# Last pass of a retention and two-MLP kernel: matmuls in the order of the source, and the squared Relu on ScalarE

## The chip, the cores and the metric

One core of one Trainium2 chip runs the whole program. The metric is device time in microseconds (us), the median of several runs.

## The reference, cut to what matters

```python
# q, k, v: (4, 8, 576, 64); 2304 tokens, width 512
ret = (scale * q @ k.T) * decay_mask        # retention, no softmax
x   = (ret @ v) -> (2304, 512)
x   = (silu(x @ w_gate) * (x @ w_val)) @ w_out     # hidden width 1536
h   = x @ w_in                                      # (2304, 2048)
g   = np.maximum(h, 0.0) ** 2                       # the squared Relu
out = g @ moe2_w_out                                # (2304, 512)
```

All matrices are float32. The kernel splits each operand into a rounded high part and a low rest, and forms each product from three matmuls (high-high, high-low, low-high).

## The kernel before, in words

After the retention, the two MLPs run in **passes** over blocks of tokens: two passes for the first, three for the second (`TOKENS`). The change touches the **last pass** of the second MLP, 768 tokens, which is the loop `for n in range(turn_over, end + 1)` (L1103).

**Systems and slots.** A pass goes through the hidden width in eight systems of 256 hidden columns. The products with `w_in` are done in Winograd-Strassen fashion: seven products instead of eight, numbered 1 to 7. One product of one system is a **slot**: six matmuls of 384 columns (`product`, L630). Products 1, 6, 7 and 4 of a system build up in one PSUM bank (`g`), 5 and 3 in another (`v`), 2 in a third (`z`). ScalarE copies a bank out between two products that share it, so product 4 can't begin before the copy after product 7 is done. The last pass has 59 slots: three that belong to the system before it, and 56 of its own. Products 7, 4 and 3 of a system stand one iteration behind its 1, 2, 6 and 5 in `seq` (L1105): 1 of n, 7 of n-1, 2 of n, 4 of n-1, 6 of n, 3 of n-1, 5 of n.

**The squared Relu** of a system stands behind products 2, 4 and 3: on 384, 384 and 768 columns. VectorE does it as one instruction, max(x, 0) times x; behind product 4, whose value lies in PSUM, ScalarE makes a Relu first.

**Block products.** In the first three pairs of systems of this pass, the second product (with `w_out`) is again done in seven products for each of three blocks of 128 tokens: 3 pairs x 3 token blocks x 7 = 63 **block products**, each six matmuls of 256 columns (`out3`, L885). Their sums of hidden blocks are four GpSimd instructions for each token block (`sums2`), which begin when the Relu behind product 3 of the pair's second system is done; `prepare` then rounds them (ScalarE, tile `hs_h`) and takes the rest (VectorE, `hs_l`). Their operands (tiles `wt`, 256 KB each) come by DMA from `operands2`. The tiles of the second pair take the place of the first pair's: a load waits until the third token block has used the tile. Block products use two PSUM banks in turn, and each bank is added into `xy` (by VectorE, or for some products of the first pair copied by ScalarE) before it is written again. The last pair of systems ends in six plain output tiles of twelve matmuls with 512 columns (`out4`; the last of them in two halves).

**Order.** Every engine executes its queue in order. The order is set when the program is built: a scheduler takes the instructions in the order of the source, and moves one ahead where, by its own estimate of times, an earlier one would have to wait. `Chained` (L109) can forbid this: while `chain["on"]` holds, each instruction of an engine is queued behind the one before it. In the kernel before this holds for the retention alone. In the last pass the source lets 1.5 block products follow each slot, from slot `begin_at` = 21 + `START` on (`flow`, L1095 and L1135), but the scheduler may place them elsewhere.

Of the kernel before, what the change touches and what calls it, by code (L numbers as in the profile page):

```python
# [13 lines left out]
AF = mybir.ActivationFunctionType  # L14
ALU = mybir.AluOpType
# [41 lines left out]
PRODUCTS = (1, 5, 6, 3, 7, 2, 4)  # L57
SUMS = (6, 5, 4, 7)
PAIRED = 6
START = 4  # L60


TINY = float(np.uint32(0x38000000).view(np.float32))
# [4 lines left out]
def retention_moe_kernel(  # L68
# [38 lines left out]
    chain = {"on": False}  # L107

    class Chained:  # L109


        def __init__(self, engine):
            self.engine, self.last, self.recent = engine, None, None

        def __getattr__(self, name):
            op = getattr(self.engine, name)

            def traced(*args, **kw):
                with ExitStack() as behind:
                    if self.last is not None:  # L120
                        behind.enter_context(tc.issue_after(self.last))
                    i = op(*args, **kw)  # L122
                self.recent = i.ins
                if chain["on"]:
                    self.last = i.ins
                return i

            return traced

    pe, dve, act, pool_e, sp = map(Chained, (nc.tensor, nc.vector, nc.scalar, nc.gpsimd, nc.sync))  # L130
# [140 lines left out]
    def bank(tag):  # L271

        turn[tag] += 1
        home = ps_g2 if late and turn[tag] % 2 else ps_g
        return home.tile([P, 512], F32, tag=tag, name=tag)
# [52 lines left out]
    def temp(tag, rows):  # L328
        return (c4_p if tag[1] == "g" else c4m_p).tile([P, rows, M1], F32, tag=tag, name=f"c{tag}", bufs=1 + (tag[1] == "g"))
# [300 lines left out]
    def product(n, dst, first, *which):  # L630

        for x, (i, o) in enumerate(which):
            w = built[n, i]
            for c in range(2):
                hi, lo = (w[:, y, c * P:(c + 1) * P] for y in range(2))
                xh, xl = (z[:, c] for z in xo[o])
                for j, (a, b) in enumerate(((hi, xh), (hi, xl), (lo, xh))):
                    at = (x * 2 + c) * 3 + j
                    pe.matmul(
                        dst, a, b, start=first and at == 0, stop=at == 6 * len(which) - 1, skip_group_check=True  # L640
                    )

    def plain_slot(n, r):
# [13 lines left out]
        if r:  # L657
            hidden(n, "c", gc)

    def slot(n, i):  # L660

        ph, p, k, what = systems[n]
        m = M[ph]
        s = sys_.setdefault(n, {})

        if i == 1 and n >= turn_over:
            s["x"] = bank("g")[:, :m]
            s["a"], s["b"] = block_tiles(n)
        elif i == 1:
            s["x"] = bank("g")[:, :m]  # L670
            s["a"] = temp("av" if what == "v" else "ag", 1 + (what != "v"))[:, :, :m]
            s["b"] = temp("bv" if what == "v" else "bg", 2)[:, :, :m]
        if i == 5:
            s["y"] = bank("v")[:, :m]
        if i == 2:
            s["z"] = ps_a.tile([P, 512], F32, tag="a0", name="z")[:, :m]
        x, a, b = s["x"], s["a"], s["b"]
        product(n, s[{2: "z", 5: "y", 3: "y"}.get(i, "x")], i in (1, 2, 5), (i, i))
        relu2 = dict(scalar=0.0, op0=ALU.max, op1=ALU.mult)
        silu = dict(func=AF.Silu)  # L680
        if what == "v":
            ga, gb = sys_[n - 1]["a"], sys_[n - 1]["b"]
        if i == 1:
            act.copy(a[:, 0], x)
        elif i == 6:
            act.copy(b[:, 0], x)
        elif i == 7:
            act.copy(b[:, 1], x)
            tt(out=b[:, 1], in0=s["y"], in1=b[:, 1], op=ALU.add)
        elif i == 2:  # L690
            tt(out=a[:, 0], in0=s["z"], in1=a[:, 0], op=ALU.add)
            if what == "g":
                act.activation(out=a[:, 0], in_=a[:, 0], **silu)
            elif what == "v":
                tt(out=ga[:, 0], in0=a[:, 0], in1=ga[:, 0], op=ALU.mult)
            else:
                dve.scalar_tensor_tensor(out=a[:, 0], in0=a[:, 0], in1=a[:, 0], **relu2)
        elif i == 4:
            if what == "g":
                act.activation(out=a[:, 1], in_=x, **silu)  # L700
            elif what == "v":
                tt(out=ga[:, 1], in0=x, in1=ga[:, 1], op=ALU.mult)
                hidden(n, "a", ga)
            else:
                act.activation(out=a[:, 1], in_=x, func=AF.Relu)
                dve.scalar_tensor_tensor(out=a[:, 1], in0=x, in1=a[:, 1], **relu2)
                hidden(n, "a", a)
        elif i == 3:
            tt(out=b[:, 0], in0=s["y"], in1=b[:, 0], op=ALU.add)
            if what == "g":  # L710
                act.activation(out=b, in_=b, **silu)
            elif what == "v":
                tt(out=gb, in0=b, in1=gb, op=ALU.mult)
                hidden(n, "b", gb)
                del sys_[n - 1], sys_[n]
            else:
                dve.scalar_tensor_tensor(out=b, in0=b, in1=b, **relu2)
                hidden(n, "b", b)
                del sys_[n]

# [2 lines left out]
    def hidden(n, which, c):  # L723
        if n >= turn_over:
            return
        kw = dict(bufs=2) if n > flip - 1 and which == "a" else {}
        hi = ho_p.tile(list(c.shape), F32R, tag=f"h{which}", name="ho_hi", **kw)
        lo = ho_p.tile(list(c.shape), F32R, tag=f"l{which}", name="ho_lo", **kw)
        split(hi, lo, c)
        hid[n, which] = hi, lo  # L730
# [67 lines left out]
    def block_tiles(n):  # L798

        k = systems[n][2]  # L800
        if k % 2 == 0:
            home = block_pools[k // 2 % 2]
            pairs_of[n] = pairs_of[n + 1] = [
                home.tile([P, 2, 2, M[2]], F32, tag=f"g{x}", name=f"ca{x}") for x in "ab"
            ]
        return [x[:, k % 2] for x in pairs_of[n]]
# [148 lines left out]
    flip, turn_over = systems.index((2, 0, 0, "i")), systems.index((2, 2, 0, "i"))  # L955
# [139 lines left out]
    def flow(upto):  # L1095
        while flowed["n"] < min(upto, len(stream)):
            follow(*stream[flowed["n"]])
            flowed["n"] += 1

    slots["n"] = 0  # L1100
    make2 = iter(())
    begin_at = 7 * 3 + START
    for n in range(turn_over, end + 1):  # L1103
        tiles = outs.get(n, [])
        seq = [(1, n), (7, n - 1), (2, n), (4, n - 1), (6, n), (3, n - 1), (5, n)]  # L1105
        if n == turn_over:
            seq = [(7, n - 1), (4, n - 1), (3, n - 1), None, (1, n), (2, n), (5, n), (6, n)]
        make = build(n + 1) if n + 1 < end else iter(())
        for x in fetch.get((n, 0), []):
            load_out(*x)  # L1110
        for x in seq:
            if x is None:
                blocks.close()
                block_pools.append(pool(ctx, "ca_p", 1, side="right"))
                t1_p = pool(ctx, "t1_p", 1, side="right")
                make2 = operands2(n + 1)
                continue
            i, k = x
            if k == end:
                continue  # L1120
            slot(k, i)
            if i == 3 and k >= turn_over and systems[k][2] % 2:
                for j in range(3):
                    if k < turn_over + PAIRED:
                        sums2(k, j)
                    queue.append((k, j))
                ready_halves()
            next(make, None)
            if tiles and (n == turn_over or i in (7, 4, 3)):
                fn, *args = tiles.pop(0)  # L1130
                fn(*args)
            slots["n"] += 1
            next(make2, None)
            past = slots["n"] - begin_at
            flow(min(int(1.5 * past + 0.7 * max(0, past - 28)), 21 * PAIRED // 2))  # L1135
            if past == 1:
                make2 = operands2(turn_over + 2)
            after(k, i)
            if n == turn_over + 1 and not tiles and t_p is None:
                second.close()  # L1140
                t_p, hl_p = pool(ctx, "t_p", 1), pool(ctx, "hl_p", 2)
                block_pools.append(pool(ctx, "cb_p", 1, side="right"))
        for fn, *args in tiles:
            fn(*args)
        for _ in make:
            pass
        if n == turn_over:
            for _ in make2:
                pass
        if n == end - 1:  # L1150
            load_last(n)
# [62 lines left out]
```

## Time and profile before

| | us |
|---|---|
| median of 3 runs | 877.3 (876.49 to 878.25) |
| the profiled execution | 876.15 |
| its span in the profile | 874.3 |
| TensorE busy in the span | 862.4 (99%) |
| VectorE busy | 675.5 (77%) |
| ScalarE busy | 415.8 (48%) |
| GpSimd busy | 172.4 (20%) |

The profiled execution took 1.85 us outside of its span. The rows of the profile call TensorE's matmuls PE, its weight loads PEld, VectorE DVE, ScalarE ACT, GpSimd POOL, and SyncE's queue of transfers SPq. All instructions go through a helper, so they all carry line 122; they are told apart by their tiles. The duration of a matmul is modelled and longer than the distance to the next one, since matmuls overlap: a wait that is shorter than this overlap doesn't show as idle time.

### The profile page before, as it was taken

To read this page: it belongs to the slowest core of one execution; us is meant where nothing else is said; L and a number is where in the kernel's file an instruction comes from. 1 tells how busy PE (TensorE), PEld (TensorE's weight loads), DVE (VectorE), ACT (ScalarE), POOL (GpSimd) and SP (SyncE) were. 2 spreads that over 40 slices of the span, in tenths; PEclk is the share of its full clock that TensorE was granted. 3 is DMA by queue.
4 is the path that set the end of the run, shared out by engine and by line. 5 is a ranking of instruction groups with operands and counts; after the bars stand their busy time and mean duration, and the time that the engine had idled before them with its cause. 6 is when DMAs were issued, how large, how long until landed. Compare 5 with 4: busy or idle time off the path is not lost.

```text
span 874.3 us, 14199 instructions
## 1 busy us (share of the span) xinstructions
PE 862.4 (99%) x5226; PEld 751.1 (86%) x5226; DVE 675.5 (77%) x1082; ACT 415.8 (48%) x756; POOL 172.4 (20%) x195
## 2 busy tenths in 40 slices
PE   8999999999999999999999999999999999999998
PEld 7878888888888888888888999889899988999986
DVE  3799999998976998778647999999654566457783
ACT  3677768564553554634335466554244232234321
POOL 3343243123220000000002311132211000062400
PEclk9999999999999999999999999999999999999999
DMA  9994867655653589878744498999989755666432
GB/s 335 402 377 158 280 231 270 243 199 174 217 197 129 175 296 365 304 252 295 249 146 156 165 338 319 357 319 385 386 286 333 250 207 157 222 236 199 164 119 72
DMA packets 87029, 217.81 MB, mean 249 GB/s; under 512 B 8752, under 2 KB 24112, under 8 KB 86960
## 3 DMA queue, kind: packets, MB, share of 16 engines
q1 hardware_dynamic: 86528, 216.50, 70.2%
q8 instruction: 41, 0.67, 0.3%
q10 hardware_dynamic: 432, 0.41, 0.1%
q14 instruction: 28, 0.23, 0.1%
HBM read 146.10 MB, written 70.78 MB: 248 GB/s over the span
## 4 chain that ended last, share of the span: by engine, by line
PE 82%; DVE 7%; DMA 7%; issue 2%; ACT 1%; SPq 0%; DVEq 0%; ACTq 0%
PE oacc L122 40%; PE g L122 24%; PE v L122 12%; PE z L122 6%; DMA k_sb<-in_kv 3%; DVE w L122 3%; DMA wt<-tsp 2%; DMA qk_sb<-in_qk 1%; DVE wi L122 1%; DVE xy L122 1%; DVE xo_l L122 1%; DMA v_sb<-in_kv 1%; DVE hs_l L122 0%; DVE cbg L122 0%; PE o L122 0%
## 5 line engine op out<-in xcount | busy, mean ns | idle before, releaser
L122 PE MATMUL g<-xo_h,wi 128*128 128x384 f32 (+1 forms) x768 | 241.3, 364 | 0.0
L122 PEld LDWEIGHTS g<-xo_h,wi 128*128 128x128 f32 x768 | 142.6, 188 | 16.8
L122 DVE TENSOR_TENSOR xy<-oacc,xy 128x512 f32<-128x512 f32 (+1 forms) x194 | 112.2, 585 | 54.2 <-PE oacc L122 53.5
L122 PE MATMUL oacc<-ho_hi,wo 128*128 128x512 f32 (+1 forms) x480 | 151.1, 370 | 0.5 <-ACT xy L122 0.5
L122 PE MATMUL g<-xo_l,wi 128*128 128x384 f32 (+1 forms) x384 | 139.7, 364 | 0.0
L122 PE MATMUL v<-xo_h,wi 128*128 128x512 f32 (+1 forms) x384 | 124.6, 364 | 0.0
L122 PE MATMUL oacc<-wo,ho_hi 128*128 128x512 f32 x384 | 119.8, 392 | 0.0
L122 PEld LDWEIGHTS oacc<-ho_hi,wo 128*128 128x128 f32 x480 | 88.1, 188 | 17.6 <-ACT xy L122 1.3
L122 PE MATMUL oacc<-ho_lo,wo 128*128 128x512 f32 (+1 forms) x240 | 89.1, 371 | 0.0
L122 PEld LDWEIGHTS oacc<-wo,ho_hi 128*128 128x128 f32 x384 | 71.5, 188 | 12.1
L122 DVE TENSOR_SCALAR w<-w 128x512 f32<-128x512 f32 (+1 forms) x136 | 65.4, 483 | 18.4 <-ACT w L122 17.4
L122 PEld LDWEIGHTS g<-xo_l,wi 128*128 128x128 f32 x384 | 72.1, 188 | 8.6
L122 PEld LDWEIGHTS v<-xo_h,wi 128*128 128x128 f32 x384 | 71.4, 188 | 8.2
L122 PE MATMUL oacc<-wo,ho_lo 128*128 128x512 f32 x192 | 74.3, 393 | 0.0
L122 PE MATMUL v<-xo_l,wi 128*128 128x512 f32 (+1 forms) x192 | 69.9, 364 | 0.0
L122 PE MATMUL z<-xo_h,wi 128*128 128x512 f32 (+1 forms) x192 | 63.0, 365 | 0.0
L122 PEld LDWEIGHTS oacc<-ho_lo,wo 128*128 128x128 f32 x240 | 45.1, 188 | 8.7
L122 ACT ACTIVATE raw<-raw 128x512 uint32<-128x512 uint16 x68 | 46.0, 677 | 13.5 <-DMA raw<-in_w 9.4
L122 DVE SCALAR_TENSOR_TENSOR w<-raw,w 128x512 uint32<-128x512 uint32 x68 | 51.2, 754 | 0.7
L122 DVE CUSTOM_DVE_ANT_0 w<-raw,w 128x1024 uint16<-128x1024 uint16 x68 | 48.7, 716 | 0.8
L122 PE MATMUL oacc<-wt,hs_h 128*128 128x256 f32 x252 | 46.9, 286 | 1.7 <-DVE xy L122 0.6
L122 DVE TENSOR_TENSOR cbg<-v,cbg 128x384 f32<-128x384 f32 (+1 forms) x56 | 34.1, 609 | 18.0 <-PE v L122 10.3
(119 smaller groups left out, 1531.6 us busy)
## 6 DMA issues: line engine op xcount, KB each, us to landing
wi<-win SPq DMA_DIRECT2D x84, 512.0 KB, 5.1
raw<-in_w SPq DMA_DIRECT2D x68, 512.0 KB, 4.8
win<-wi SPq DMA_DIRECT2D x60, 512.0 KB, 3.8
wo<-wsp SPq DMA_DIRECT2D x32, 512.0 KB, 6.0
wsp<-wo SPq DMA_DIRECT2D x28, 512.0 KB, 5.3
qk_sb<-in_qk SPq DMA_DIRECT2D x15, 576.0 KB, 7.2
wst<-w SPq DMA_DIRECT2D x32, 256.0 KB, 6.2
wi<-win SPq DMA_DIRECT2D x28, 256.0 KB, 5.9
```

The source lines that it names most:

```text
L122: i = op(*args, **kw)
```

## The change

Three things change together, all in the last pass:

- every TensorE instruction of the pass is queued behind the one before it in the source (`pe.on`)
- the squared Relu there is two ScalarE instructions, Relu and Square (`square`); VectorE has none of it
- block products begin two slots later in the source (`START` 4 to 6), and the pace at which they follow the slots is written otherwise

```diff
-START = 4
+START = 6
...
-                if chain["on"]:
+                if chain["on"] or self.on:
                     self.last = i.ins
...
+    def square(n, dst, src):
+        late_ = n >= turn_over
+        if late_ or src is not dst:
+            act.activation(out=dst, in_=src, func=AF.Relu)
+        if late_:
+            act.activation(out=dst, in_=dst, func=AF.Square)
+        else:
+            dve.scalar_tensor_tensor(out=dst, in0=src, scalar=0.0, in1=dst, op0=ALU.max, op1=ALU.mult)
...
-                dve.scalar_tensor_tensor(out=a[:, 0], in0=a[:, 0], in1=a[:, 0], **relu2)
+                a0 = a[:, 0]
+                square(n, a0, a0)
...
-                act.activation(out=a[:, 1], in_=x, func=AF.Relu)
-                dve.scalar_tensor_tensor(out=a[:, 1], in0=x, in1=a[:, 1], **relu2)
+                square(n, a[:, 1], x)
...
-                dve.scalar_tensor_tensor(out=b, in0=b, in1=b, **relu2)
+                square(n, b, b)
...
     slots["n"] = 0
+    pe.on, pe.last = True, pe.recent
...
             past = slots["n"] - begin_at
-            flow(min(int(1.5 * past + 0.7 * max(0, past - 28)), 21 * PAIRED // 2))
+            flow(min(int(1.5 * past + 0.25 * max(0, past - 14) + 0.45 * max(0, past - 26)), 21 * PAIRED // 2))
```

## Rows read from the trace of the kernel before

**Rows 1.** The page, part 1: busy time of each engine and its share.

```profile
PE 862.4 (99%) x5226; PEld 751.1 (86%) x5226; DVE 675.5 (77%) x1082; ACT 415.8 (48%) x756; POOL 172.4 (20%) x195
```

**Rows 2.** Stages of the last pass: length, busy time (instructions) of each engine, clock, DMA.

```profile
718.20:780.00 61.80, 61.80 (x332) 57.41 (x331) 35.87 (x52) 19.16 (x36) 9.91 (x12) 1.00 0.62 206
780.00:833.30 53.30, 52.31 (x360) 51.45 (x359) 37.49 (x67) 19.08 (x39) 19.82 (x24) 1.00 0.56 182
833.30:871.00 37.70, 36.17 (x230) 31.65 (x228) 23.12 (x46) 7.18 (x12) 0.00 (x0) 1.00 0.26 86
871.00:874.30 3.30, 0.00 (x0) 0.00 (x0) 0.40 (x1) 0.00 (x0) 0.00 (x0) 1.00 0.26 77
```

**Rows 3.** One tile's instructions in a stretch: `wi`; `wt`; `wo`; `wt` from 833.3.

```profile
765.50:871.00 105.50, 41.14 (x218) 36.91 (x216) 0.00 (x0) 0.00 (x0) 1.00 0.48 160
...
765.50:871.00 105.50, 51.30 (x378) 48.37 (x378) 1.00 0.48 160
...
765.50:871.00 105.50, 17.50 (x84) 14.05 (x84) 0.00 (x0) 0.00 (x0) 0.00 (x0) 1.00 0.48 160
...
833.30:871.00 37.70, 18.93 (x144) 17.67 (x144) 1.00 0.26 86
```

**Rows 4.** The chain that ended last, in order of time: start, length, what.

```profile
789.94 2.09 PE g L122 x12
792.02 1.42 PE oacc L122 x12
...
802.31 7.16 DMA wt<-tsp
...
809.53 7.30 DMA wt<-tsp
```

**Rows 5.** Timeline of PE: start, length, instruction, matmuls merged, idle time before.

```profile
816.11 0.28 PE L122 MATMUL oacc<-wt,hs_l 128*128 128x256 f32 x1
816.88 0.38 PE L122 MATMUL oacc<-wt,hs_h 128*128 128x256 f32 x1 [0.49 <-DMA wt<-tsp]
...
858.13 0.63 PE L122 MATMUL oacc<-wo,hs_h 128*128 128x512 f32 x2
...
858.83 0.63 PE L122 MATMUL oacc<-wo,hs_h 128*128 128x512 f32 x2
```

**Rows 6.** Timeline of four engines: from slot product 3 to the first block sums.

```profile
763.27 0.33 PE L122 MATMUL v<-xo_h,wi 128*128 128x384 f32 x1
...
765.00 0.95 DVE L122 SCALAR_TENSOR_TENSOR cab<-cab 128x768 f32<-128x768 f32 x1
...
767.68 1.05 POOL L122 TENSOR_TENSOR xy<-cab 128x256 f32<-128x256 f32 x1
...
769.58 0.73 POOL L122 TENSOR_TENSOR xy<-cab 128x256 f32<-128x256 f32 x1
...
773.06 2.89 POOL L122 TENSOR_TENSOR xy<-caa,xy 128x256 f32<-128x256 f32 x3
...
774.58 2.00 ACT L122 CAST hs_h<-xy 128x1024 fp32r<-128x1024 f32 x2 [0.66 <-POOL xy L122]
...
775.67 1.36 DVE L122 TENSOR_TENSOR hs_l<-xy,hs_h 128x1024 fp32r<-128x1024 f32 x1 [1.72 <-ACT hs_h L122]
```

**Rows 7.** Instruction groups of one shape: count, busy us, mean ns, idle before.

```profile
L122 DVE SCALAR_TENSOR_TENSOR cab<-cab 128x768 f32<-128x768 f32 x8 | 7.6, 956 | 0.2
L122 DVE SCALAR_TENSOR_TENSOR caa<-caa 128x384 f32<-128x384 f32 x8 | 5.3, 662 | 0.1
...
L122 ACT CAST xo_h<-xy 128x768 fp32r<-128x768 f32 x4 | 3.3, 834 | 2.4 <-DVE xy L122 1.6 <-PE v L122 0.8
L122 ACT ACTIVATE caa<-g 128x384 f32<-128x384 f32 x8 | 3.9, 493 | 10.7 <-PE g L122 10.7
...
L122 ACT ACT_TABLE_LOAD x2 | 2.6, 1283 | 2.2 <-issue 2.2
```

**Rows 8.** Waits of SP's queue from 765.5: sum, times, longest.

```profile
SPq L122 <- PE oacc L122: 31.4, 13, 8.7
```

More of the change, by code (lines that the diff above doesn't have):

```diff
@@ L112, in __init__ @@
         def __init__(self, engine):
-            self.engine, self.last, self.recent = engine, None, None
+            self.engine, self.last, self.recent, self.on = engine, None, None, False
         def __getattr__(self, name):
@@ L678, in slot @@
         product(n, s[{2: "z", 5: "y", 3: "y"}.get(i, "x")], i in (1, 2, 5), (i, i))
-        relu2 = dict(scalar=0.0, op0=ALU.max, op1=ALU.mult)
         silu = dict(func=AF.Silu)
```

## The prediction

> **What bounds the kernel now.** I read the page's first part, then busy time by stage, then the last pass on TensorE's own timeline. TensorE is busy for 99% of the span [rows 1], so only two things can change the time: the amount of its work, and the time in which it stands still. The change leaves its work alone; the question is what it stands still for, before and after. In the last pass it shows no idle time up to 780, then 1.0 us to 833.3 and 1.5 us to 871; the 3.3 us behind that are the last addition and its store [rows 2]. These idle times understate the loss, because a matmul's modelled end lies behind the start of the next. So I count the loss by starts. Twelve matmuls of 384 columns take 2.09 us, 0.174 each, and twelve of 256 take 1.42, 0.118 each [rows 4]; three of 512 take 0.70, 0.233 each [rows 5]. From 765.5 there are 216 of the first kind (36 slots; the row shows two more that began at its edge), 378 of the second (all 63 block products), and 84 in the output tiles, of which 60 have 512 and 24 have 256 columns [rows 3]. Work: 216 x 0.174 + (378 + 24) x 0.118 + 60 x 0.233 = 37.6 + 47.4 + 14.0 = 99.0 us. It runs from 765.5 to about 870.8, 105.3 us. **Lost: 6.3 us.** I put it at 6.1, since waits alone count. Of this, the tail from 833.3 holds the most: 144 matmuls of block products [rows 3], which is 24 of the 63, and the output tiles make 17.0 + 2.8 + 14.0 = 33.8 of 37.5 us, so 3.7 are lost there and some 2.4 before it. One such loss is seen at 816.88: the matmul starts 0.77 us after the one before it, where 0.12 is normal, behind a transfer of `wt` [rows 5].
>
> **The change part by part.** *The order.* By the source, 55 block products stand ahead of slot 59, with the old pace (past = 34: 51 + 0.7 x 6) as with the new (past = 32: 48 + 4.5 + 2.7). The scheduler had put only 39 there, and 24 into the tail. In the order of the source 8 are left for the tail. That moves no work away, but a block product between slots has a slot's 1.04 us more until its bank is needed again, and one in the tail has only the 0.71 us of its neighbour. With 8 in place of 24 in the tail, the 3.7 us lost there would shrink to 1.2 in proportion; the products of neighbouring token blocks are also no longer mixed, so that rounding of the next block can begin one block product group earlier. I take 0.8, bounds 0 and 1.5.
>
> *The start of the block products* is where the new order can cost. The second block product needs a sum that hangs on slot product 3 of the second system (slot 20). Block product 1 follows slot 28 (21 + 6 + 1) and the second follows slot 29. From the modelled end of slot 20's last matmul that is nine slots and one block product, 9.4 + 0.7 less the 0.16 us of overlap: TensorE arrives after 9.95 us. The chain that it needs: an addition of 384 columns (0.6 with its wait, by the 384-column row of VectorE), Relu and Square on 768 columns (0.83 each by ScalarE's rounding of that size [rows 7]), 0.2 of hand-overs, so GpSimd starts at 2.5. It started 2.35 us after that matmul in the trace [rows 6] (763.60 to 765.95), so the second ScalarE step costs nothing beyond what VectorE's queue cost there. Then GpSimd: its twelve instructions were queued with the three token blocks interleaved, so the first block's sums were complete only with the tenth. ScalarE could round them at 774.58, 8.6 us after 765.95 [rows 6]. Some of those instructions took 1.05 us and others 0.73 [rows 6]; ten at 0.72 would be 7.2. Then 1.05 for rounding, and the rest 1.3 later, of which 0.24 hides. So TensorE waits 2.5 + 7.2 + 1.05 - 9.95 = 0.8 for the high part and 1.05 more for the low one, 1.9 us in all; with 8.6 it is 3.3, and with the blocks one after the other (four instructions, 2.9) the chain is done at 7.8 and nothing waits. In the kernel before other slots were put into this gap, which the new order forbids. I take 2.0, bounds 0 and 3.3: nearest to the undisturbed rows, because VectorE loses its squaring. Rows show the longer GpSimd instructions while such VectorE work ran at 765.00 and just after [rows 6]. The Trainium skill (GPSIMD Engine Reference, Specifications) says that GpSimd shares its SBUF interfaces with VectorE and contends with VectorE instructions that have two SBUF inputs; the squaring is one. By that rule alone the wait is 1.9, without it 3.3; the trace agrees as far as 1.05 against 0.73 us goes.
>
> *Operands of the next pair.* A `wt` tile is loaded again when the third token block has used it. Between that and its next use the source has about four slots and five block products, 4.2 + 3.5 + 0.4 = 8.1 us. Two such transfers took 7.16 and 7.30 us from release to use [rows 4]. That fits with half a microsecond to spare; bounds 0 and 1.5 (twice the 0.65 us lost at 816.88), taken 0.5.
>
> *Product 7 to product 4.* Without block products between them only one slot, 1.04 us, covers ScalarE's copy: 0.16 of overlap, about 0.1 to start, 0.5 for 384 columns [rows 7]. This leaves some 0.3, and two or three times the copy may stand behind a Relu or Square of 0.83 us: 0 to 1, taken 0.2.
>
> *Squared Relu.* VectorE loses 8 instructions of 0.96 and 16 of at most 0.66 us, some 18 us. ScalarE gains five of them for each system, 2 x 0.83 + 3 x 0.49 = 3.1 us, 25 in all. It was busy 45 of 153 us [rows 2], so both lie under TensorE and cost nothing by themselves; without this cover, on a chain that TensorE waits for, each square would cost 0.1 (behind product 4) to 0.7 us (behind 3).
>
> **The sum.** New waits 2.0 + 0.5 + 0.8 + 0.2 = 3.5, old ones 6.1: 2.6 us less. The profiled execution took 876.15 (span 874.3 and 1.85 around it), so 873.55. That execution was 1.15 below the median of 877.3; against the median I forecast **874.7 us**. From no change I count what differs by over 0.2%, 1.75 us, about what a measurement of this kernel can tell.
>
> **Rivals.**
> - *The waits go altogether.* The sums are ready in time, and the tail runs through: new waits 0.5 to 1. 877.3 - 5.5 = 871.8 us. For it: the bounds of 0 above. Against: the interleaved sums were seen [rows 6].
> - *They only move.* At the first block products 3.3, and the other terms at their upper bounds of 1.5, 1.5 and 1: 7.3 in place of 6.1, 878.5; halfway there, 876 to 878: no change. That the scheduler's order was already that of the source I rule out nearly (39 products against 55); it would give 877.3.
> - *Slower: one late transfer.* SP issues transfers in order, and its queue stood up to 8.7 us for a block product [rows 8]. TensorE may no longer pass over a block product whose `wt` is late. If a load stands 8.7 us behind another's wait, its half microsecond of slack leaves 8.2 us of standing still: 877.3 + 8.2 - 2.6 = 882.9. It decides from 4.4 us of such lateness on (2.6 + 1.75). Against: by the source the loads stand in the order in which tiles come free.
> - *Slower: function tables.* A load of ScalarE's tables took 1.28 us, and there were two in the whole kernel [rows 7], none between the Silu and the Relu that the last pass used already. If Square needed other tables than Relu and copy, each of 24 Squares would bring two loads, 62 us on ScalarE, and a copy that has 0.3 us to spare would stand behind them: at 1 us each, 877 + 24 = some 900. The Trainium skill (ScalarE: Activation LUTs, Table sets) says that functions lie in sets, and that a switch of set costs a load of about 1283 ns and a DRAIN; cheap functions are in every set, where its list names relu, copy, identity and abs but not square. No row of this trace has a Square.
>
> **How the numbers follow.** Forecast 0.50, waits gone 0.14, only moved 0.20 (with the order unchanged in it), a late transfer 0.14, tables 0.02. Of the forecast's half, 0.04 lies above 875.55, the bound of no change, and of the moved case 0.01 above 879.05. So faster 0.60, same 0.23, slower 0.17. The range leaves out the last two cases and little of the second: 871.9 to 878.7. The likeliest case's own range is 873 to 876.
>
> **What would show it.** In the timeline of the changed kernel: slots and block products strictly alternating, 8 block products behind the last slot in place of 24; a wait of about 2 us at the second block product, released by `hs_h` or `hs_l`; less than 1 us lost in the tail; GpSimd's instructions near 0.73; no squaring on VectorE; two table loads as now. I am wrong if the first wait is over 4 us, if PE waits several times for `wt`, or if a third table load appears.

## The result, and the profile after

| | before | after |
|---|---|---|
| median, us | 877.58 (876.49 to 878.25, 4 runs) | 884.62 (884.3 to 885.68, 4 runs) |
| the profiled execution / its span | 876.15 / 874.3 | 884.61 / 882.8 |

The changed kernel is **slower**: ratio 1.0084, 95% interval 1.0066 to 1.0101. I had forecast 874.7 us, a range of 871.9 to 878.7, and given "slower" 0.17.

Busy time of the whole kernel after the change, as in [rows 1]:

```profile
PE 864.4 (98%) x5226; PEld 752.5 (85%) x5226; DVE 657.5 (74%) x1058; ACT 437.8 (50%) x796; POOL 168.3 (19%) x195
```

The work moved as planned: VectorE lost 18 us, ScalarE gained 22, TensorE's instructions are as many as before. The stages, with the same columns as [rows 2]:

```profile
718.20:780.00 61.80, 57.12 (x294) 51.65 (x292) 28.60 (x42) 27.43 (x48) 8.70 (x12) 1.00 0.62 200
780.00:833.30 53.30, 49.05 (x340) 47.84 (x341) 26.64 (x48) 26.04 (x53) 13.08 (x17) 1.00 0.51 168
833.30:879.50 46.20, 45.75 (x296) 42.23 (x294) 26.51 (x52) 15.72 (x26) 5.06 (x8) 1.00 0.34 104
```

Where [rows 2] showed no idle time up to 780 and 1.0 us to 833.3, 4.7 and 4.25 us are now idle; the tail has 0.45 in place of 1.5. As in the prediction, idle time alone understates the loss, so I also count by starts: in the profiled execution, how much later than at the normal pace (0.174, 0.119 and 0.232 us behind a matmul of 384, 256 and 512 columns) each matmul of the last pass starts, summed. This "lost" time is **5.8 us before and 12.4 after**, in four stretches:

| lost, us | 718 to 765 | 765 to 800 | 800 to 833.3 | from 833.3 |
|---|---|---|---|---|
| before | 0.1 | 1.4 | 0.9 | 3.6 |
| after | 0.1 | 8.7 | 2.5 | 1.6 |

So the tail gained 2 us (I expected 2.9, from 3.7 to 0.8), and 765 to 833.3 gave back 8.9. (The stretches are counted each with its own pace; they add up to 0.2 and 0.5 more than the whole.) The two spans differ by 8.5 us, of which 1.9 arose ahead of this pass: matmul 4301, in order of start, begins at 716.2 before and at 718.1 after. That leaves 6.6 us for the last pass, as the count does (12.4 - 5.8). The view of waits says for what TensorE stood still from 718 on, in us, times, longest:

```profile
PE g L122 <- ACT caa L122: 3.7, 2, 2.9
PE g L122 <- DMA wi<-win: 3.1, 1, 3.1
PE oacc L122 <- ACT hs_h L122: 0.8, 1, 0.8
PE oacc L122 <- DVE hs_l L122: 0.8, 1, 0.8
PE oacc L122 <- DMA wt<-tsp: 0.4, 1, 0.4
PE oacc L122 <- DVE xy L122: 0.3, 1, 0.3
```

Before, the longest such wait was 0.5 us. The places, on TensorE's timeline (columns as in [rows 5]):

```profile
772.69 0.44 PE L122 MATMUL g<-xo_h,wi 128*128 128x384 f32 x1 [3.12 <-DMA wi<-win]
...
778.65 0.50 PE L122 MATMUL oacc<-wt,hs_h 128*128 128x256 f32 x2 [0.80 <-ACT hs_h L122]
779.91 0.38 PE L122 MATMUL oacc<-wt,hs_l 128*128 128x256 f32 x1 [0.76 <-DVE hs_l L122]
...
790.26 0.45 PE L122 MATMUL g<-xo_h,wi 128*128 128x384 f32 x1 [2.90 <-ACT caa L122]
```

I call them **A** (772.69), **B** (778.65 and 779.91) and **C** (790.26, and once more 1.0 us at 823.01). The chain that ended last, in order of time, shows what stands behind each:

```profile
764.39 8.25 DMA wi<-win
...
772.69 1.31 PE g L122 x6
774.00 1.05 PE v L122 x6
...
775.08 0.57 DVE cab L122
...
775.67 0.85 ACT cab L122
...
776.55 0.85 ACT cab L122
777.39 0.26 ACT xy L122
777.65 0.95 ACT hs_h L122
...
778.63 1.24 DVE hs_l L122
```

*A.* Product 3 of the second system ends at 764.37 and frees a tile of `wi`. The load into it is issued at once and lands 8.25 us later. Product 6 of the fourth system needs it, and in the written order only five slots (5.2 us) lie between. So TensorE stands for 8.25 - 5.2 = 3.05 us, and 0.06 for the two hand-overs. The free order of the kernel before had other slots and twelve matmuls of block products to put there.

*B.* The second block product waits for the rounding of its sums. That cast ran only at 777.65: behind Relu, Square (`cab`) and a copy in ScalarE's queue, which had themselves waited for product 3 of the third system, late by A.

*C.* ScalarE's timeline around 790:

```profile
787.27 0.62 ACT L122 CAST hs_h<-caa 128x512 fp32r<-128x512 f32 x1
787.80 0.52 ACT L122 ACTIVATE caa<-caa 128x384 f32<-128x384 f32 x1
788.22 0.35 ACT L122 COPY xy<-oacc 128x256 f32<-128x256 f32 x1
788.48 0.40 ACT L122 CAST hs_h<-cab 128x256 fp32r<-128x256 f32 x1
788.78 1.04 ACT L122 CAST hs_h<-xy 128x1024 fp32r<-128x1024 f32 x1
789.73 0.48 ACT L122 COPY caa<-g 128x384 f32<-128x384 f32 x1
```

Product 6 of the fifth system can't begin before product 1 is copied out of its bank into `caa` (789.73). This `caa` still holds the first pair's hidden values, until the third token block is rounded (787.27). The rounding needs a pair of `hs` tiles, of which there are two; one comes free when the first token block's seventh block product is done, at 787.25. Since block products now begin two slots later, so does this release, and the copy stands behind it in ScalarE's queue.

### The profile page after: what moved, and what is told of

Its sections match the earlier page's. It is cut to its first block, busy times and chain, and to the rows that moved or that the text cites. A ratio compares the mean times of both kernels' runs of the same rounds, so it can differ in the third digit from the quotient of the medians.

```text
span 882.8 us, 14205 instructions
## 1 busy us (share of the span) xinstructions
PE 864.4 (98%) x5226; PEld 752.5 (85%) x5226; DVE 657.5 (74%) x1058; ACT 437.8 (50%) x796; POOL 168.3 (19%) x195
## 4 chain that ended last, share of the span: by engine, by line
PE 83%; DMA 7%; DVE 6%; ACT 2%; issue 1%; SPq 0%; DVEq 0%
PE oacc L122 40%; PE g L122 23%; PE v L122 12%; PE z L122 6%; DVE w L122 3%; DMA qk_sb<-in_qk 2%; DMA wt<-tsp 2%; PE o L122 2%; DMA v_sb<-in_kv 1%; PE s L122 1%; DMA wi<-win 1%; DMA raw<-in_w 1%; DVE wi L122 1%; DVE xy L122 1%; PE kv L122 1%
## 5 line engine op out<-in xcount | busy, mean ns | idle before, releaser
L122 PEld LDWEIGHTS oacc<-wo,ho_hi 128*128 128x128 f32 x384 | 71.5, 188 | 12.4
```

## The experiments

Each batch ran beside the kernel before on the same chip; its medians were 876.7 to 877.5. "Lost" is that of the profiled execution's last pass. That execution isn't always near the median: it took 889.03 with the order fixed from slot 28, 882.87 with the squares alone and 882.55 with START 4.

| run | median, us | ratio, 95% interval | lost, us |
|---|---|---|---|
| fixed order alone | 886.76 | 1.0102 (1.0073 to 1.0131) | 14.2 |
| squares on ScalarE alone | 880.64 | 1.0042 (1.0025 to 1.0059) | 9.8 |
| START and pace alone | 877.96 | 1.0012 (1.0001 to 1.0024) | 6.4 |
| order, START and pace | 887.35 | 1.0114 (1.0093 to 1.0135) | 16.8 |
| change, 3 ahead of 6 | 878.98 | 1.0015 (1.0001 to 1.0030) | 6.6 |
| change, START 4 | 884.90 | 1.0077 (1.0051 to 1.0103) | 11.8 |
| change, fixed from slot 28 | 885.77 | 1.0083 (1.0057 to 1.0110) | 15.7 |
| before, fixed from slot 57 | 879.84 | 1.0024 (1.0011 to 1.0038) | 7.9 |
| change, 6 last | 877.47 | 0.9995 (0.9982 to 1.0007) | 5.4 |
| change, 6 last, START 8 | 880.48 | 1.0035 (1.0022 to 1.0048) | 9.3 |
| 3 ahead of 6, squares on VectorE | 880.18 | 1.0039 (1.0021 to 1.0057) | 9.1 |
| before, 3 ahead of 6 | 878.33 | 1.0014 (1.0001 to 1.0027) | 6.8 |
| change, sums in order | 884.87 | 1.0075 (1.0048 to 1.0101) | 13.5 |
| change, 6 last, sums in order | 877.01 | 0.9994 (0.9980 to 1.0009) | 4.7 |
| the same, copies on VectorE | 875.53 | 0.9977 (0.9961 to 0.9993) | 4.1 |
| before, sums in order | 875.68 | 0.9982 (0.9967 to 0.9997) | 3.6 |
| before, sums in order, squares on ScalarE | 877.81 | 1.0007 (0.9991 to 1.0022) | 5.6 |
| before, sums in order, 6 last | 878.25 | 1.0007 (0.9992 to 1.0022) | 5.3 |

**The parts of the change.** The first four undo parts of it. My theories were A, the fixed order makes the loss, and B, ScalarE's queue does (in these four expectations the letters name theories, not the waits).

```diff
# fixed order alone: START 4, old pace, and squares on VectorE
-        late_ = n >= turn_over
+        late_ = False
# squares alone: START 4, old pace, and no fixed order
-    pe.on, pe.last = True, pe.recent
# START and pace alone: both of these edits, START 6 and the new pace
# order, START and pace: late_ = False alone
```

> TensorE's matmuls of the last pass in the order of the source; squared Relu on VectorE and the block products' pace as before. Theory A (the fixed order makes the loss: a slot waits for a wi load, the first block products for their sums, a slot for ScalarE's copy into a hidden tile that an earlier pair still occupies): 3 to 7 us slower than before, 880.5 to 884.5, with single PE waits of 2 to 3.5 us between 768 and 795. Theory B (the loss is ScalarE's queue, which got 25 us of Relu and Square): 873 to 877, no wait over 1.5 us.

> Squared Relu of the last pass in two ScalarE instructions; order left to the scheduler, pace as before. Theory A: within 1 us of before, 876.5 to 878.5. Theory B: 4 to 7 us slower, 881.5 to 884.5.

> Only START 6 and the new pace; order left to the scheduler, squares on VectorE. Both theories: within 1.5 us of before, since the scheduler moves block products anyway; if it is slower by over 2 us, the later start is a cause of its own.

> Order of the source and the new pace, squares on VectorE: the change without its ScalarE part. Theory A: 4 to 7 us slower than before, 881.5 to 884.5, close to the whole change. Theory B: 873 to 876. A value between, 878 to 881, would say that both share the loss.

The fixed order alone costs 1.0%, START and pace 0.1%, the squares alone 0.4%. The order alone, and order with pace, lie 2.3 and 2.9 us above even theory A's ranges. The order alone has the waits A (3.0 us) and B (2.7), and no C. Much of the rest is TensorE's clock: between 765 and 800 the granted clock was 0.85 in the profile of the order alone and 0.90 with order and pace, where the changed kernel had 1.00. Over the whole span, three executions of the order alone at a clock of 0.993 to 0.995 took 886.75 to 887.17, and one at 0.999 took 881.49; with order and pace, three at 0.996 took 886.72 to 887.97, and one at 1.000 took 883.90. By these executions 3 to 5 us of the two medians is the lower clock, which came in or just behind the waits.

The parts don't add up: with order and pace in place, the squares on ScalarE seem to give back 2.7 us (887.35 to 884.62, though the two intervals overlap) instead of costing 3.7. But at a clock of 1.000 the two kernels took 883.90 and 884.30, one execution each, so the 2.7 us may be the clock alone. Neither theory holds alone, but the order is the largest part.

The 2 us that the tail gained need both edits. From 833.3 on, 3.9 and 3.5 us are lost in the two runs with the fixed order and squares on VectorE, 4.0 with the squares on ScalarE and a free order, 3.6 before, and 1.6 with both. These stretches hold unlike work, since in the fixed order the last slots run until 854 to 857. Behind the last slot alone, 3.5 us are lost before, 1.8 in both runs with the fixed order and squares on VectorE, 3.7 with the squares alone, and 0.8 with both edits. The waits of the run with order and pace, whose matmuls stand in the same written order as the changed kernel's, are for VectorE's additions, and a square stands ahead of them in VectorE's queue, of 384 columns (and the rest of 1024 columns before it) at the first and of 768 at the second:

```profile
855.03 0.51 PE L122 MATMUL oacc<-wt,hs_h 128*128 128x256 f32 x2 [0.79 <-DVE xy L122]
859.04 0.50 PE L122 MATMUL oacc<-wt,hs_h 128*128 128x256 f32 x2 [0.55 <-DVE xy L122]
```

```profile
852.96 1.22 DVE L122 TENSOR_TENSOR hs_l<-xy,hs_h 128x1024 fp32r<-128x1024 f32 x1
854.10 0.55 DVE L122 SCALAR_TENSOR_TENSOR caa<-g,caa 128x384 f32<-128x384 f32 x1
...
857.70 0.96 DVE L122 SCALAR_TENSOR_TENSOR cab<-cab 128x768 f32<-128x768 f32 x1
858.58 0.75 DVE L122 TENSOR_TENSOR xy<-oacc,xy 128x256 f32<-128x256 f32 x2
```

In the run with the squares alone TensorE shows one long wait, for a transfer, and nothing of ScalarE:

```profile
817.74 0.50 PE L122 MATMUL oacc<-wt,hs_h 128*128 128x256 f32 x2 [3.44 <-DMA wt<-tsp]
```

That transfer took 9.37 us, where two like it took 7.16 and 7.30 [rows 4]; behind the wait TensorE ran at the lower clock for 3.4 us.

**Short distances in the written order.** From here on, theory C says that each wait is a distance in that order that is too short; theory D, that the order has no slack anywhere, so that what is won at one place is lost at the next.

```diff
# change, 3 ahead of 6
-        seq = [(1, n), (7, n - 1), (2, n), (4, n - 1), (6, n), (3, n - 1), (5, n)]
+        seq = [(1, n), (7, n - 1), (2, n), (4, n - 1), (3, n - 1), (6, n), (5, n)]
# change, 6 last
+        seq = [(1, n), (7, n - 1), (2, n), (4, n - 1), (3, n - 1), (5, n), (6, n)]
# change, START 4: with the old pace
-START = 6
+START = 4
# change, fixed from slot 28 (57 in the other run, with START 4, old pace, squares on VectorE)
-    pe.on, pe.last = True, pe.recent
...
             slots["n"] += 1
+            if slots["n"] == 28:
+                pe.on, pe.last = True, pe.recent
```

> The whole change, with product 3 of the system before put one slot ahead of product 6 in each iteration (order 1, 7, 2, 4, 3, 6, 5). Theory C (each wait is a distance in the written order that is too short): the tile wi1 that product 3 frees is needed by product 6 seven slots later instead of five, 2.1 us more, so the 3.3 us wait at 772.7 falls to about 1.2; the sums behind product 3 begin one slot earlier, so the 2.0 us at the second block product fall to about 1.0; product 6 of the fifth system comes one slot later, so the 3.1 us at 790.3 fall to about 2.0. Together 4 us less than the whole change: about 880.6. Theory D (the order has no slack anywhere, so time won at one place is lost at the next): waits in other places grow, total within 1.5 us of the whole change, 883 to 886.

The first gave 5.6 us back, more than the 4 expected. Its waits:

```profile
773.24 0.44 PE L122 MATMUL g<-xo_h,wi 128*128 128x384 f32 x1 [1.63 <-DMA wi<-win]
777.74 0.50 PE L122 MATMUL oacc<-wt,hs_h 128*128 128x256 f32 x2 [0.36 <-ACT hs_h L122]
779.00 0.38 PE L122 MATMUL oacc<-wt,hs_l 128*128 128x256 f32 x1 [0.76 <-DVE hs_l L122]
789.35 0.44 PE L122 MATMUL g<-xo_h,wi 128*128 128x384 f32 x1 [0.43 <-ACT caa L122]
```

A fell by 1.5 rather than 2.1 (its transfer took 8.84 us this time), C by 2.5 and its second wait of 1.0 is gone, the others fell by a little.

> The whole change, with products in the order 1, 7, 2, 4, 3, 5, 6: product 3 is as early as in the run with 3 ahead of 6, and product 6 is one slot later still. Theory C: the wait for wi1 falls by one more slot, from 1.8 us to about 0.8; the two at the second block product stay at 1.4 together, since product 3 has not moved; the wait for caa, 0.6, goes. Together 1.6 us less than with 3 ahead of 6: about 877.4. Theory D: product 6 now stands only one slot ahead of product 7 of its system, and the copy out of the bank between them waits behind the squares: several waits of 0.3 to 1 us, 879 or more.

With product 6 one slot later still, the time was 877.47 for 877.4 expected, and A and C are gone from its timeline. B stayed (1.0 and 1.0, for 1.4 expected), and a new wait of 1.3 came at 798.06:

```profile
773.63 0.50 PE L122 MATMUL oacc<-wt,hs_h 128*128 128x256 f32 x2 [0.84 <-ACT hs_h L122]
775.01 0.39 PE L122 MATMUL oacc<-wt,hs_l 128*128 128x256 f32 x1 [0.88 <-DVE hs_l L122]
798.06 0.51 PE L122 MATMUL oacc<-wt,hs_h 128*128 128x256 f32 x2 [1.13 <-ACT xy L122]
```

So two products moved in the written order, with nothing else touched, take away the whole loss of the change.

> The whole change, but block products begin two slots earlier (START 4, with the old pace). Theory C: the wait for wi at 772.7 stays at 3.3; the wait at the second block product grows by two slots, from 2.0 to about 4; the wait of product 6 of the fifth system for the copy into caa falls by as much, from 3.1 to about 1, and the 1.0 us at 823 goes; total 0 to 1 us below the whole change, 883.5 to 885. Theory D: the sum of the waits grows with the earlier start, 886 to 888, since nothing of the first wait is given back.

C vanished, B grew to 3.4 us and A stayed at 3.1, as theory C says (about 4 was expected for B). The total was within its 883.5 to 885, but in part by luck: A, B and C together are 2.8 us shorter than in the changed kernel, and a granted clock of 0.51 between 776.3 and 783.2 took most of that back. START trades one wait for another:

```profile
771.04 0.44 PE L122 MATMUL g<-xo_h,wi 128*128 128x384 f32 x1 [2.93 <-DMA wi<-win]
776.58 0.80 PE L122 MATMUL oacc<-wt,hs_h 128*128 128x256 f32 x2 [2.46 <-ACT hs_h L122]
777.84 0.58 PE L122 MATMUL oacc<-wt,hs_l 128*128 128x256 f32 x1 [0.47 <-DVE hs_l L122]
```

> The same order 1, 7, 2, 4, 3, 5, 6, with block products beginning two slots later still (START 8). Theory C: the waits at the second block product (1.4) go; the wait for caa comes back, since the first group of block products ends two slots later: 2.1 us less the slack of about 0.4, so 1.6. The two edits cancel: within 1 us of the run with START 6, 876.5 to 878.5. If the copy into caa has more slack than that, about 876.

In this kernel the second pair's sums stand in the source ahead of the rounding of a token block of the first pair, which is then computed from the wrong sums; the amount of work is the same. B went and C came back, 2.0 us for 1.6 expected. The total of 880.48 lies 2 us above the bound, with a new wait of 1.6 us for `hs_l` at 830.69, so it doesn't confirm the sum.

> The whole change, but the fixed order of TensorE begins only behind the 28th slot, where the block products begin; the slots ahead of it are free to be moved. Theory C: the wait for wi1 at 772.7 (3.3 us) is the only one that goes, since the scheduler can put other slots ahead of product 6; the waits at the second block product (2.0) and for caa (3.1) stay: about 881.3. Theory D: the time comes back at the second block product, which is reached 3 us earlier while its sums are no earlier: about 884.

> The kernel before, with one thing added: the fixed order of TensorE from slot 57 of the last pass on (squares on VectorE, START 4 and the old pace as before). Theory C: none of the three places with a short distance lies there, so no wait of over 1 us is added; the tail is in order and loses about 1 us less than before: 875 to 877. Theory D: a fixed order of even these last slots costs more than it saves: 878 to 880.

For theory C both were misses. With the order fixed from slot 28 on, A shrank to 0.6, but B grew to 3.3 and C stayed; the rest is TensorE's clock (below). This is what theory D says of B. Fixing the order from slot 57 on, with the squares on VectorE, made the kernel before slower by 0.2%, as theory D expected; from 833.3 on it lost 5.5 us for 3.6, in six waits of 0.35 to 0.9 us and smaller ones. The fixed order is thus no gain in the tail by itself.

> The kernel before with only the order of products 3 and 6 changed (no fixed order, START 4, squares on VectorE). Theory C: the scheduler already fills the gap in front of product 6 with other slots, so the distance costs nothing there: 876 to 878, no change. If the short distance also cost the kernel before something (a share of the 2.4 us lost ahead of 833), it gains up to 2 us: 875.

With a free order the same exchange gains nothing (1.0014): the scheduler had covered A already.

> Product 3 ahead of product 6, the fixed order and START 6 with the new pace, but the squares on VectorE as before. With the old order of products, moving the squares to ScalarE was worth 2.7 us (887.35 against 884.62). If that came from TensorE's clock, which fell to the lower level behind the long waits of the kernel with squares on VectorE, it vanishes here, where no wait is over 2 us: 878 to 880. If VectorE itself was late, the 2.7 us stay: 881 to 882.

880.18 lies just above the 878 to 880 of the clock, 1.2 us above the run with squares on ScalarE, within the two intervals. The profiles' tails differ as above, 4.5 us lost for 1.5 from 833.3 on, without a fall of the clock in either, so the clock is not all that the squares were worth.

**The order of the sums.** GpSimd's queue is put in the source's order, so that the first token block's four sums come first.

```diff
     slots["n"] = 0
+    pool_e.on, pool_e.last = True, pool_e.recent
# copies on VectorE
         if k == 1 and i in (1, 5, 6, 4):
-            act.copy(home, src)
+            dve.tensor_copy(out=home, in_=src)
```

> The whole change, with GpSimd's instructions of the last pass also queued in the source's order, so that the four sums of the first token block come first instead of mixed with those of the other two. If the 2.0 us at the second block product come from the mixing: the first block's sums are done after 2.9 instead of 7.2 us, both waits there go, and the rest stays (3.3 for wi1, 3.1 for caa): about 882.6. If they come from ScalarE's queue (rounding behind Relu, Square and a copy): no change, 884 to 885.

B went completely, and yet the time stayed. TensorE's two remaining long waits, and the three windows behind them (length, busy times, granted clock as the third number from the end):

```profile
771.97 0.45 PE L122 MATMUL g<-xo_h,wi 128*128 128x384 f32 x1 [3.19 <-DMA wi<-win]
789.02 0.45 PE L122 MATMUL g<-xo_h,wi 128*128 128x384 f32 x1 [2.90 <-ACT caa L122]
```

```profile
772.00:775.00 3.00, 3.00 (x11) 3.00 (x12) 0.47 (x1) 1.31 (x2) 3.00 (x4) 0.62 0.35 143
775.00:778.00 3.00, 3.00 (x17) 3.00 (x17) 1.69 (x2) 1.27 (x4) 0.87 (x2) 0.81 0.44 119
790.00:793.00 3.00, 3.00 (x15) 3.00 (x14) 0.31 (x1) 1.68 (x4) 0.00 (x0) 0.50 0.00 0
```

The same windows of the changed kernel ran at a granted clock of 1.00. The lost time is 13.5 against 12.4, with the 1.9 us of B gone, so some 3 us went to the lower clock.

> Product order 1, 7, 2, 4, 3, 5, 6 with the same order of GpSimd's sums. If the mixing is the cause, the two waits of 1.0 us at the second block product go: 877.47 - 2.0 = 875.5, below the kernel before. If ScalarE's queue is the cause: 877.5.

> As the run before, and the block products of the first pair that ScalarE copies out of PSUM are copied by VectorE. If ScalarE's queue is what made TensorE wait 1.3 us at 798.1 for the copy into xy, that goes too: about 874.2. If VectorE is as late, no gain against the run before: 875.5.

With product 6 last, no such waits are left. B went here as well; part of its 2.0 us came back as a wait of 1.0 for `xy` behind ScalarE and two for `wt` (1.0 at 810.15 and 0.6 at 811.51), and the median fell by 0.5 only. With the copies on VectorE the wait behind ScalarE went too, and 875.53 is below the kernel before.

> The kernel before with GpSimd's instructions of the last pass in the source's order and nothing else. If the free order of TensorE already covers late sums: no change, 876.5 to 877.5. If the early sums also spare the kernel before some of the 2.4 us that it loses ahead of 833: about 876.

The smallest edit does as well: the kernel before, with the sums alone in order, took 875.68, and its lost time between 765 and 833.3 fell from 2.3 to 0.2 us. The free order had paid for the mixed sums too.

> No fixed order of TensorE; squares on ScalarE as in the change, GpSimd's sums in the source's order, START 4 and the old pace. If the 3.7 us of the squares alone were the one late transfer of wt, set off by where TensorE then stood: it need not come again, and the run is near the kernel before with sums in order, 875.7 to 877. If ScalarE's longer queue costs by itself: 875.7 + 3.7 = 879.4.

> The kernel before with the sums in order (875.7) and the products in the order 1, 7, 2, 4, 3, 5, 6, no fixed order of TensorE, squares on VectorE. If the free order covers the wait for wi1 anyway: no further gain, 875 to 877. If the longer distance also helps here: about 874.

Without the late transfer, the squares still cost 2.1 us against 875.68 (877.81), between the two answers expected; 1.9 of the lost time came back between 800 and 833.3, with no wait over 0.7 us. Product 6 last gains nothing under a free order: 878.25.

## Why the prediction was wrong

- **What failed: the list of new waits.** It had four terms (3.5 us). The largest two of the real ones, A (3.3 us) and C (4.1), are not among them: they were put at nothing. Two edits to the order remove both and the loss with them. I looked at reloads for `wt`, from release to next use, but not at those for `wi`, whose pace the free order had set; and at product 7 to product 4, but not at the buffer (`caa`) that the copies go into. The same count of slots would have given some of A from the trace before. There the loads of `wi` between 760 and 780 took up to 7.1 us, which five slots don't cover by 1.9; that the load in question would take 8.25 it doesn't show.

```profile
DMA to landing us min/median/max: 3.4/4.6/7.1
```

- *The start of the block products*, 2.0, measured 1.9. The size was right by luck, the route only in part. TensorE came 3 us later than I had worked out, because of A, and the sums alone would then have been in time: GpSimd began at 766.79, 2.4 us behind the slot (2.5 forecast), and its tenth instruction ended near 774.1 (7.3 us, 7.2 forecast), as here:

```profile
768.40 0.91 POOL L122 TENSOR_TENSOR xy<-cab 128x256 f32<-128x256 f32 x1
769.28 0.72 POOL L122 TENSOR_TENSOR xy<-caa,cab 128x256 f32<-128x256 f32 x1
...
771.32 2.09 POOL L122 TENSOR_TENSOR xy<-xy,caa 128x256 f32<-128x256 f32 x3
773.38 2.12 POOL L122 TENSOR_TENSOR xy<-caa,xy 128x256 f32<-128x256 f32 x3
```

  But the rounding had missed its place in ScalarE's queue. That the mixing is the root was shown: with the sums in order B is gone. The instructions of 1.05 us [rows 6] are down to 0.91 and 0.95, and most take 0.72. The rule of the Trainium skill (GPSIMD Engine Reference, Specifications), that GpSimd contends with VectorE's instructions with two SBUF inputs, agrees with the trace: the two long ones ran beside the rests `hs_l<-cab,hs_h` (767.42 to 768.72), and one beside `caa<-z` (769.11), whose `z` lies in PSUM, took 0.72. The square at 765.00, to which the prediction put it down, had ended before the first sum, and in the trace before both a later square and rests ran beside the long ones; what the squaring alone does is not shown apart.
- *Operands of the next pair*, 0.5: right, 0.5 us at 819.78.
- *The order in the tail*, 0.8: behind the last slot, for which it was worked out, 0.8 is lost, for 3.5 before; from 833.3 on it is 1.6, for 3.6. The size was right, the reason half: I put the gain down to the order, from 24 block products to 8 behind the last slot (in the trace it is 10: the count of 55 has in it the two that follow slot 59). The order alone brings 3.5 to 1.8 there, and nothing from 833.3 on (3.5 to 3.9); VectorE's additions, freed from the squares that stood ahead of them, made the rest.
- *Product 7 to product 4*, 0.2: no wait of that kind shows among TensorE's waits. C, 3.1 + 1.0, is the term that should have stood there.
- *Squared Relu*, nothing: wrong both ways. In the fixed order squares on ScalarE are a gain in the tail (1.6 against 3.5 us lost from 833.3 on, 1.5 against 4.5); in the medians it is 878.98 against 880.18, within the intervals, and 884.62 against 887.35, which the clock blurs. In the free order they cost 3.7 and 2.1 us, and why is open. In the first of these last two the profile shows a late transfer of `wt` and the lower clock behind it; in the second it shows no single cause.
- *The rivals.* The late transfer was right that TensorE can't pass over what is late, and wrong in its place: `wi` was issued on time, and landed late by itself. That its 882.9 lies near the measured time is luck. The tables can be excluded: there are two loads, as before. The list of functions in every set in the Trainium skill (ScalarE: Activation LUTs, Table sets) does not name square; no set was loaded for it here.

```profile
L122 ACT ACT_TABLE_LOAD x2 | 2.6, 1283 | 2.2 <-issue 2.2
```

The balance: between 765 and 833.3, A 3.3, B 1.9, C 4.1 and 1.9 of smaller losses stand in place of 2.3, which is 8.9 more; the tail has 2.0 less. The lost time rises by 6.6 when it is counted over the whole pass, close to the 7.0 us of the medians. The prediction had 6.1 lost before, for 5.8 here, so its base was sound, and what it lacked stands in the new waits.

## What to carry to other kernels

Before an engine's order is fixed, follow every buffer that it reads or fills, weights and copies too, from release to next use, and count what the written order puts between; a free order may have been covering a distance that looks harmless in its trace. When such a wait appears, first try to move the release earlier or the use later by a slot or two: here two products moved were worth 7 us, while later starts only traded waits. And look at which of several interleaved results is needed first: putting it first was one line, and gained 0.2% in the kernel before, though nothing in the changed one.

## What the runs showed of the hardware

The granted clock of TensorE fell to 0.5, its level of 1.2 GHz, for 3.4 us at a time, twice that in three cases, in the last pass of seven of the profiles. Each fall came in or just behind a single wait of 1.9 to 3.4 us: with sums in order (0.62 and 0.50 above), with the order alone, with order and pace, with the order fixed from slot 28, with START 4, with START 8, and with the squares alone, where the pace of 256 columns was 0.21 us in place of 0.12. In the changed kernel's profile the waits of 3.1 and 2.9 us had no such fall behind them. With sums in order some 3 us were lost in two falls, so a wait of this length may cost half as much again or not; what decides it these runs don't show.

The load of `wi`, 512 KB, took 8.25 us in the changed kernel and 8.84 with 3 ahead of 6, with the DMA engines busy for 0.99 and 0.91 of the time, where the whole kernel's median for its kind is 4.9. That share alone doesn't set the time: in the kernel before, one issued at 763.63 took 7.08 us with the engines busy for 1.00 of it.

```profile
wi<-win SPq DMA_DIRECT2D x84, 512.0 KB, 4.9
```

Executions differ by up to 3 us long before the last pass: matmul 1001, in order of start, begins between 66.7 and 69.7 us in the twenty profiles. A count of lost time within the pass leaves this out, and a single execution's time does not.
